# A reordered start, reordered steps, and a unit's scores and outputs placed on either side of one product

## The chip, the cores and the metric

The kernel runs on one core of a Trainium2 chip. The metric is the device time of one execution in microseconds. Three runs of the kernel before gave 498.42 (median), 497.5 and 498.45.

## The reference, cut to what matters

Two stages follow each other. The first is a linear attention with a decaying state, for 4 sequences of 768 tokens and 8 heads of 48 channels:

```python
for t in range(S):
    cur = einsum('bhd,bhe->bhde', u[None] * kt, vt)
    y[:, :, t] = einsum('bhd,bhde->bhe', rt, state + cur)
    state = w[None, :, :, None] * state + einsum('bhd,bhe->bhde', kt, vt)
```

The second takes its output as x (3072 tokens of 384 channels) and computes g = elu(x @ w_in) with 2048 hidden channels, and then g @ w_out. All is in float32.

## The kernel before, in words

**Units and layers.** The tokens are cut into chunks of 128. A *unit* (n, b) is chunk n (0 to 5) of sequence b (0 to 3). In a unit the recurrence is written as matrix products: scores (k by r, both scaled by powers of w, masked), the diagonal with u, outputs (scores by v, plus r by the state) and the state that is handed on. The four units of a chunk give the 512 columns of x for a *layer* n of the second stage. A layer has 16 steps f, one for each 128 hidden channels: `hidden` multiplies x by w_in (L1198), `negative` and `elu` apply the nonlinearity, `split_g` splits g, and `project` multiplies by w_out (L1254; L1241 in the last layer). Float32 accuracy is kept by splitting x, g and the weights into a high part in a fast format and the rest, so that each product is three matmuls for each of three chunks, nine of 512 columns.

**Ahead of the branch.** `prepare` loads w and u and the first r, k and v, runs some matmuls on ones (`warm`, L486), turns w into a column by small matmuls (`by_channels`, L490, copied at L495), finds its smallest and largest value (L109, L110), from which a flag says whether the fast path is allowed (L111, L113), and forms the powers of w (L132). These instructions are put in order by the framework's planner. All engines then read the flag and branch.

**START.** In the fast path the order is written out by hand: each engine executes its instructions in the order in which the program issues them, and `START` is the list of short names that `start` goes through, for layer 0's own units and the first weights. For instance `Lk:3` loads k of unit 3, `rud:1` forms r u k of unit 1 on VectorE (L730, L731; without the d on POOL), `sum` sums it (L742), `krd` or `kr` multiplies k by its decays (L749), `Tr` and `Tk` transpose on TensorE (L635), `dr`, `dra`, `dk`, `tka` take the transposes out of PSUM, `A` is the scores (L772), `m0` and `m1` their masking (L694), `tl`, `tla`, `tld` copy the tails of v (L840), `vd` and `vdd` form v times the diagonal (L852), `O` and `V` are outputs (L869, L879), `xh` and `xl` split them into x (L888, L890), `wm` is warming matmuls (L500), and `H:0`, `H:1` are the first half (256 columns) of the first two products by w_in. `Lw` loads a tile of weights.

**The weights** come as float32 and are rounded by integer steps: `wd` (L574) and `lb` (L580) on ScalarE, `ma` (L588) and `mb` (L596), called merges here, on VectorE, the cast `sp` (L616) on ScalarE, the rests `r3` and `r4` (L626) on POOL. In layer 0 every step does this for the tile of two steps later.

**The steps.** `step` goes through `FIRST` in layer 0 and `LATER` in all others. Names with a last hexadecimal digit belong to a unit's *stage*: a unit of the next layers starts every four steps, and the digit says in which step of its life (4 to 11 for units of chunk 1, 4 to 9 for the others) the operation is issued. `ru` and `kr` and `sum` are as above; `t` transposes blocks on VectorE (L647), `m` moves them through DRAM (L656, L661), `br` (POOL, L670) and `bk` (ScalarE, L679) take them; units of chunk 1 use TensorE (`T`, `dr`, `tka`) instead. `D` puts the diagonal into the scores' tile (POOL, L976), `A` is the scores and the states' products (L921, L935), `pa` and `pb` copy the two halves of the scores under the mask (VectorE, L983), `ss` forms the two state sums (L945, L948), `Y` is the outputs (L999, L1007), `xy` (ScalarE, L1018), `xa` (VectorE, L1027), `xh` (ScalarE, L1034) and `xl` (L1036) bring them into x, `sw` decays the state (POOL, L951), `G` fills x by DMAs (L1112), and `rk` and `v` ask for the inputs of the unit after next. `proj` is the product by w_out of g of two steps before (of one step before up to step (1,3), so that step (1,4) has none). Behind the last one of a layer VectorE transposes the banks with the results (L1262).

Scores and outputs of a unit use the same two PSUM banks in turn, so outputs wait until the masked scores and the state sums have been taken out. All loads and stores are issued by SP, in order.

Of the kernel before, what the change touches and what calls it, by code (L numbers as in the profile page):

```python
# [18 lines left out]
B, H, S, D = 4, 8, 768, 48  # L19
# [13 lines left out]
FILL = DP - D  # L33
FILLS = [slice(i * DP + D, (i + 1) * DP) for i in range(2)]
W_LOW, W_HIGH = 0.8, 1.2
WARM = 6
EARLY = (1, 4)

DEEP, WIDE = 3, 2

START = """
inv tb ub Lv:1 Lk:3 wm:4 kt Tr:0 rud:1 kr:1 Tr:1 Tk:0 tl:1 dra:1 Lr:3 rud:0 Lw:0 dr:0 sum:1 sum:0 Tk:1 tka:1
dk:0 S:1 wd:0 tla:0 A:1 A:0 Tr:3 rud:3 Lk:2 Lr:2 kr:3 m0:1 m1:1 Tr:2 Tk:3 Lw:2 m1:0 vdd:1 rud:2 O:1 Lw:1 kr:0
m0:0 tka:3 vd:0 O:0 V:0 kr:2 Tk:2 Lv:3 wd:1 dr:3 lb:0 dr:2 Lw:4 sum:2 lb:1 sum:3 ma:0 xh:0 V:1 Lw:5 mb:0 Lw:3
A:3 ma:1 xh:1 xl:1 Lv:2 xl:0 tka:2 mb:1 m1:3 S:3 tla:2 S:0 lb:2 m0:3 tld:3 vdd:2 A:2 Ln:1 m1:2 vd:3 O:3 sp:1
S:2 wd:2 sp:0 m0:2 O:2 V:3 xh:3 V:2 wm:1 Lw:6 Ln:0 rsd:1 xh:2 ht rsd:2 rsd:0 xl:3 H:0 Lw:7 xl:2 Lw:8 H:1 wm:2
"""

FIRST = """
D9 ma rud8 rka ru4 wd lb hid A9 bk7 kr8 mb T8 neg m6 sum6 Ya sum8 t5 xya sp pa9 xaa kr4 br6 xha elu va dr8 pb9 r3 gh tka8 ss9 xlda D7 Gb swb proj gl Lw r4  # L50
"""
LATER = """
hid t5 Y9 A8 br7 pa8 D6 proj rud4 xy9 neg xa9 elu pb8 xh9 gh bk7 kr4 m5 ss8 xl9 rk8 gl v9 G9 sum5 sw9
"""


class Kernel:
# [12 lines left out]
    def prepare(self, ctx):  # L70
        nc, tc = self.nc, self.tc
        cp = ctx.enter_context(tc.tile_pool(name="cp", bufs=1))

        self.rev = cp.tile([P, H, DP], F32, tag="rev", name="rev")
        self.state = [cp.tile([P, HP, DP], F32, tag=f"state{b}", name=f"state{b}") for b in range(B)]
        early = self.rev.rearrange("p h d -> p (h d)")
        w_row = early[0:1, 0:DM]
        nc.sync.dma_start(w_row, self.w.rearrange("(o h) d -> o (h d)", o=1))

        self.w_col = w_col = cp.tile([P, 8 * HP], F32, tag="w_col", name="w_col")[:, :HP]  # L80
        nc.vector.memset(w_col, 1.0)

        self.slots = [
            (
                cp.tile([P, H, DP], F32, tag=f"r_t{i}", name=f"r_t{i}"),
                cp.tile([P, H, DP], F32, tag=f"k_t{i}", name=f"k_t{i}"),
                cp.tile([P, H, DP], F32, tag=f"v_t{i}", name=f"v_t{i}"),
            )
            for i in range(2)
        ]  # L90
        self.ident = cp.tile([P, P], F32, tag="ident", name="ident")
        make_identity(nc, self.ident)
        ones = early[:, DM:]
        nc.vector.memset(ones, 1.0)
        self.raw = {}
        for b in range(2):
            self.raw[0, b] = self.slots[b]
            self.clear_pads(self.slots[b])
        self.load_rk(0, 0, (0,))
        self.u_b = cp.tile([P, H, D], F32, tag="u_b", name="u_b")  # L100
        self.u_row, self.one = early[DP : DP + 1, 0:DM], ones[DP : DP + 1, :]
        nc.sync.dma_start(self.u_row, self.u.rearrange("(o h) d -> o (h d)", o=1))
        self.load_rk(0, 0, (1,))
        self.load_rk(0, 1)
        self.load_v(0, 0)


        lim = self.lim = cp.tile([1, 48], F32, tag="lim", name="lim")[:, 0:4]
        nc.vector.tensor_reduce(lim[:, 0:1], w_row, axis=AX.X, op=ALU.min)  # L109
        nc.vector.tensor_reduce(lim[:, 1:2], w_row, axis=AX.X, op=ALU.max)  # L110
        nc.vector.tensor_single_scalar(out=lim[:, 2:3], in_=lim[:, 0:1], scalar=W_LOW, op=ALU.is_ge)  # L111
        self.flag = cp.tile([1, 1], I32, tag="flag", name="flag")
        nc.vector.scalar_tensor_tensor(  # L113
            self.flag, lim[:, 1:2], W_HIGH, lim[:, 2:3], op0=ALU.is_le, op1=ALU.mult
        )

        self.warm(WARM, w_row, ones)


        self.mask = cp.tile([P, P], F32, tag="mask", name="mask")  # L120
        nc.gpsimd.memset(self.mask, 1.0)
        nc.gpsimd.affine_select(
            out=self.mask, in_=self.mask, pattern=[[1, P]], compare_op=ALU.is_gt,
            fill=0.0, base=0, channel_multiplier=-1,
        )
        for t in self.state:
            nc.gpsimd.memset(t, 0.0)
        self.pw = cp.tile([P, HP, P + 1], F32, tag="pw", name="pw")
        nc.vector.memset(self.pw[:, :, 0:1], 1.0)

        for a in range(HP):
            nc.vector.tensor_tensor_scan(  # L132
                self.pw[:, a, 1 : P + 1], w_col[:, a : a + 1].to_broadcast([P, P]), ones,
                1.0, op0=ALU.mult, op1=ALU.mult,
            )

        self.pairs = []
        for k in range(NF + 1):
            self.pairs.append([
                cp.tile([P, self.count(k), DM], F32R, tag=f"{n}{k}", name=f"{n}{k}")  # L140
                for n in ("wh", "wl")
            ])
# [335 lines left out]
    def warm(self, times, w_row, ones):  # L478

        with self.tc.tile_pool(name="ps_w", bufs=1, space=PSUM) as ps:  # L480
            junk = ps.tile([P, P], F32, tag="junk", name="junk")
            col = ps.tile([P, HP], F32, tag="col", name="ps_col")
            for i in range(times):
                if i == 2:
                    self.by_channels(col, w_row, ones[0:1, 0:1], self.w_col)
                self.nc.tensor.matmul(junk, lhsT=ones, rhs=ones, start=True, stop=True)  # L486

# [804 lines left out]
@with_exitstack  # L1292
def rwkv_elu_ffn(ctx: ExitStack, tc: tile.TileContext, r, k, v, w, u, w_in, w_out, out):
    nc = tc.nc
    kn = Kernel(tc, r, k, v, w, u, w_in, w_out, out)
    kn.prepare(ctx)

    near_one = nc.values_load(kn.flag, min_val=0, max_val=1)
    with tc.If(near_one > 0) as cmp:
        kn.arm(general=False)  # L1300
    with cmp.Else():
        kn.arm(general=True)
# [30 lines left out]
```

## Time and profile before

| what | before |
| --- | --- |
| median of 3 runs | 498.42 us |
| profiled execution | 498.74 us |
| its span | 497.0 us |
| TensorE matmul busy | 482.9 us (97%) |
| VectorE busy | 288.7 us (58%) |
| ScalarE busy | 253.7 us (51%) |
| POOL busy | 152.7 us (31%) |
| all DMA queues, share of 16 engines | 40.3% and 0.7% |

The span runs from the first to the last instruction of the profiled execution; 1.74 us lie around it. Busy shares are means over stages with different limits: VectorE is busy for 9 tenths and more in some slices up to 110 us and for 4 to 6 tenths later. A busy TensorE includes the time in which a matmul passes through its pipeline, so the starts of the matmuls are read where times between them matter.

### The profile page before, as it was taken

The page shows a single profiled execution, that of the slowest core. Times are in us where ns is not written, and L with a number is a line of the kernel's source. Part 1 is how long each engine was busy: PE and PEld are TensorE (multiplying, and loading weights), DVE is VectorE, ACT ScalarE, POOL GpSimd, SP SyncE. Part 2 cuts the span into 40 slices and gives each one's busy share as a digit, 9 for nine tenths or more (in the row PEclk, how much of TensorE's full clock was granted, in tenths as well). Part 3 has the DMA queues.
Part 4 walks back from the last instruction along what each step waited for, and adds up shares of the span by engine and source line. Part 5 has one row for each costly group of instructions (what it writes and reads, how often), then busy time and mean ns, then how long its engine had stood idle before and what let it go on. Part 6 is the DMA issues. An engine that isn't in the chain of part 4 may idle for free.

```text
span 497.0 us, 11551 instructions
## 1 busy us (share of the span) xinstructions
PE 482.9 (97%) x4650; PEld 398.7 (80%) x4650; DVE 288.7 (58%) x506; ACT 253.7 (51%) x454; POOL 152.7 (31%) x169
## 2 busy tenths in 40 slices
PE   8899999999999999999999999999999999999995
PEld 7787877777878888788888788888788888899995
DVE  6988898995565455554454654554754633433332
ACT  2459988863543544444444444445435435444442
POOL 4457769573331322322313303313302201000000
PEclk9999999999999999999999999999999999999998
DMA  7977666733444533434434434534434300020002
GB/s 161 237 176 179 188 176 165 171 103 96 122 95 115 141 74 85 119 90 120 122 84 98 113 76 120 139 64 104 119 73 124 94 17 11 11 54 0 1 0 71
DMA packets 109955, 51.06 MB, mean 103 GB/s; under 512 B 89026, under 2 KB 105796, under 8 KB 109892
## 3 DMA queue, kind: packets, MB, share of 16 engines
q1 hardware_dynamic: 109892, 50.22, 40.3%
q8 instruction: 39, 0.64, 0.6%
q14 instruction: 24, 0.20, 0.1%
HBM read 35.13 MB, written 13.11 MB: 97 GB/s over the span
## 4 chain that ended last, share of the span: by engine, by line
PE 78%; DVE 11%; ACT 4%; issue 2%; POOL 2%; DMA 1%; SPq 0%; DVEq 0%; ACTq 0%
PE ps_h L1198 32%; PE ps_acc L1254 27%; PE ps_acc L1241 7%; DVE wide L596 3%; DVE wide L588 3%; PE ps_y L999 2%; PE ps_a L921 2%; PE ps_y L1007 2%; PE ps_a L935 1%; ACT wh L616 1%; DVE ps_h L1213 1%; PE ps_y L869 1%; DVE g L1221 1%; ACT g L1219 1%; DMA r_t<-in_r_dram 1%
## 5 line engine op out<-in xcount | busy, mean ns | idle before, releaser
L1198 PE MATMUL ps_h<-x,wh 128*128 128x512 f32 (+1 forms) x588 | 174.6, 386 | 0.4 <-DMA x<-x 0.4
L1254 PE MATMUL ps_acc<-g,wh 128*128 128x512 f32 x480 | 167.1, 401 | 1.4 <-DVE g L1221 0.8
L1198 PEld LDWEIGHTS ps_h<-x,wh 128*128 128x128 f32 x588 | 109.5, 188 | 22.2 <-issue 0.8
L1213 DVE SCALAR_TENSOR_TENSOR ps_h<-g,ps_h 128x512 f32<-128x512 f32 x96 | 66.5, 693 | 93.3 <-ACT g L1208 93.3
L1198 PE MATMUL ps_h<-x,wl 128*128 128x512 f32 (+1 forms) x294 | 108.8, 387 | 0.8 <-POOL wl L626 0.8
L1254 PEld LDWEIGHTS ps_acc<-g,wh 128*128 128x128 f32 x480 | 89.9, 188 | 23.6 <-DVE stage L1262 1.8
L1207 ACT ACTIVATE g<-ps_h 128x512 f32<-128x512 f32 x96 | 57.6, 600 | 82.6 <-PE ps_h L1198 82.5
L1219 ACT CAST g<-ps_h 128x512 fp32r<-128x512 f32 x96 | 56.3, 587 | 76.7 <-DVE ps_h L1213 76.7
L1254 PE MATMUL ps_acc<-g,wl 128*128 128x512 f32 x240 | 93.8, 391 | 0.0
L1221 DVE TENSOR_TENSOR g<-ps_h,g 128x512 fp32r<-128x512 f32 x96 | 66.2, 689 | 46.2 <-ACT g L1219 45.9
L1198 PEld LDWEIGHTS ps_h<-x,wl 128*128 128x128 f32 x294 | 55.0, 188 | 12.9 <-POOL wl L626 2.1
L1208 ACT ACTIVATE g<-g 128x512 f32<-128x512 f32 x96 | 60.7, 633 | 3.1
L749 POOL TENSOR_TENSOR k_t<-k_t,rev 128x384 f32<-128x384 f32 x22 | 24.5, 1117 | 99.2 <-DVE ru L731 92.6
L1254 PEld LDWEIGHTS ps_acc<-g,wl 128*128 128x128 f32 x240 | 45.1, 188 | 8.1
L1036 POOL TENSOR_TENSOR x<-x_f,x 128x512 fp32r<-128x512 f32 x16 | 20.7, 1295 | 91.2 <-ACT x L1034 91.2
L626 POOL TENSOR_TENSOR wl<-wide,wh 128x384 fp32r<-128x384 f32 x29 | 35.8, 1254 | 16.1 <-ACT wh L616 16.1
L983 DVE COPY_PREDICATED a<-mask,ps_a 128x256 f32<-128x256 int32 x40 | 17.8, 444 | 31.8 <-PE ps_a L935 30.8
L1018 ACT COPY x_f<-ps_y 128x256 f32<-128x256 f32 x40 | 12.9, 374 | 43.9 <-PE ps_y L1007 43.9
L1241 PE MATMUL ps_acc<-wh,g 128*128 128x384 f32 x128 | 35.0, 337 | 0.0
L670 POOL TENSOR_TENSOR rk<-rk,pw 128x512 f32<-128x512 f32 x16 | 19.0, 1189 | 35.3 <-DMA rk<-blocks 33.5
L1241 PEld LDWEIGHTS ps_acc<-wh,g 128*128 128x128 f32 x128 | 23.4, 188 | 0.6
L976 POOL TENSOR_TENSOR a<-ident_h,diag 128x512 f32<-128x512 f32 x20 | 21.6, 1080 | 6.7 <-DVE diag L742 6.3
(127 smaller groups left out, 478.7 us busy)
## 6 DMA issues: line engine op xcount, KB each, us to landing
blocks<-tb SPq DMA_DIRECT2D x64, 128.0 KB
rk<-blocks SPq DMA_DIRECT2D x16, 512.0 KB
stage<-in_moe_w_out_dram SPq DMA_DIRECT2D x16, 384.0 KB
stage<-in_moe_w_in_dram SPq DMA_DIRECT2D x32, 144.0 KB
r_t<-in_r_dram SPq DMA_DIRECT2D x22, 192.0 KB
k_t<-in_k_dram SPq DMA_DIRECT2D x22, 192.0 KB
v_t<-in_v_dram SPq DMA_DIRECT2D x22, 192.0 KB
out_dram<-stage SPq DMA_DIRECT2D x80, 48.0 KB
```

What stands on the lines that cost most here:

```text
L626: (eng or self.nc.gpsimd).tensor_sub(lo, a, hi.bitcast(F32))
L749: (eng or self.nc.gpsimd).tensor_mul(k, k, self.rev[:, :, 0:D])
L976: self.nc.gpsimd.tensor_mul(un["a"], self.ident_h.unsqueeze(1).to_broadcast([P, H, DP]), un["diag"].unsqueeze(2).to_broadcast([P, H, DP]),)
L1036: (eng or nc.gpsimd).tensor_sub(x[:, 1], xf, x[:, 0].bitcast(F32))
L1198: self.nc.tensor.matmul(ph[:, part], lhsT=a[:, c * P : (c + 1) * P], rhs=x[:, c, part], start=(i == 0), stop=(i + 1 == len(todo)),)
L1207: nc.scalar.activation(g, ph, AF.Relu, scale=-1.0)
L1208: nc.scalar.activation(g, g, AF.Exp, scale=-1.0)
L1213: self.nc.vector.scalar_tensor_tensor(ph, g, -1.0, ph, op0=ALU.add, op1=ALU.max)
L1219: nc.scalar.copy(part, g)
L1221: nc.vector.tensor_sub(part, g, self.g[n, f][2].bitcast(F32))
L1241: self.nc.tensor.matmul(self.acc[n][b][:, 0:DM], lhsT=a[:, at], rhs=w, start=(f == 0 and i == 0), stop=(f == NF - 1 and i == 2),)
L1254: self.nc.tensor.matmul(self.acc[n][c], lhsT=w[:, c * P : (c + 1) * P], rhs=g, start=(f == 0 and i == 0), stop=(f == NF - 1 and i == 2),)
```

## The change

In `prepare` the order is now the written one too, `warm` stands ahead of the compare and the flag, and has 4 matmuls on ones instead of 6, two of them ahead of the column of w. `START`, `FIRST` and `LATER` hold other orders. In `LATER` the scores `A8` stand ahead of the product by w_in (`hid`) and the outputs `Y8` behind it in the same step; before, scores stood behind the product, and outputs (`Y9`) behind the product of the next step. The block transposes and moves (`t`, `m`) and `bk` go one stage earlier, `rk` one stage later.

```diff
--- before.py
+++ after.py
@@ -33,24 +33,27 @@
 FILL = DP - D
 FILLS = [slice(i * DP + D, (i + 1) * DP) for i in range(2)]
 W_LOW, W_HIGH = 0.8, 1.2
-WARM = 6
+WARM = 4
+FIRST_WARM = 2
 EARLY = (1, 4)
 
 DEEP, WIDE = 3, 2
 
 START = """
-inv tb ub Lv:1 Lk:3 wm:4 kt Tr:0 rud:1 kr:1 Tr:1 Tk:0 tl:1 dra:1 Lr:3 rud:0 Lw:0 dr:0 sum:1 sum:0 Tk:1 tka:1
-dk:0 S:1 wd:0 tla:0 A:1 A:0 Tr:3 rud:3 Lk:2 Lr:2 kr:3 m0:1 m1:1 Tr:2 Tk:3 Lw:2 m1:0 vdd:1 rud:2 O:1 Lw:1 kr:0
-m0:0 tka:3 vd:0 O:0 V:0 kr:2 Tk:2 Lv:3 wd:1 dr:3 lb:0 dr:2 Lw:4 sum:2 lb:1 sum:3 ma:0 xh:0 V:1 Lw:5 mb:0 Lw:3
-A:3 ma:1 xh:1 xl:1 Lv:2 xl:0 tka:2 mb:1 m1:3 S:3 tla:2 S:0 lb:2 m0:3 tld:3 vdd:2 A:2 Ln:1 m1:2 vd:3 O:3 sp:1
-S:2 wd:2 sp:0 m0:2 O:2 V:3 xh:3 V:2 wm:1 Lw:6 Ln:0 rsd:1 xh:2 ht rsd:2 rsd:0 xl:3 H:0 Lw:7 xl:2 Lw:8 H:1 wm:2
+Lk:3 inv Lv:1 Lr:3 tb ub kt rud:1 Tr:0 sum:1 krd:1 Tr:1 tl:1 Tk:0 dra:1 rud:0 dr:0 vdd:1 Tk:1 tka:1 Lw:0 dk:0
+S:1 wd:0 lb:0 tld:0 A:1 Lr:2 A:0 wm:2 Lk:2 Tr:3 sum:0 rud:3 m0:1 m1:1 Tr:2 kr:3 Lw:1 Tk:3 m0:0 rud:2 m1:0 kr:0
+O:1 kr:2 O:0 vd:0 Lw:2 sum:2 V:0 Tk:2 dr:3 Lv:3 Lw:4 dr:2 tka:3 Lw:3 lb:1 V:1 ma:0 mb:0 wd:1 A:3 ma:1 tka:2
+xh:1 sum:3 xl:1 Lv:2 xh:0 Lw:6 mb:1 xl:0 lb:2 sp:1 m1:3 S:0 m0:3 tl:3 Lw:5 S:3 tla:2 A:2 vdd:2 m1:2 Ln:1 vd:3
+Ln:0 S:2 m0:2 O:3 O:2 V:3 wd:2 V:2 sp:0 ht xh:3 rsd:2 Lw:7 rsd:0 xh:2 rsd:1 wm:2 H:0 xl:3 H:1 Lw:8 xl:2
 """
 
 FIRST = """
-D9 ma rud8 rka ru4 wd lb hid A9 bk7 kr8 mb T8 neg m6 sum6 Ya sum8 t5 xya sp pa9 xaa kr4 br6 xha elu va dr8 pb9 r3 gh tka8 ss9 xlda D7 Gb swb proj gl Lw r4
+
+D9 lb ma ru4 hid wd Ya A9 neg rud8 t5 mb xya xaa sp elu ss9 kr8 kr4 pb9 bk7 rkb pa9 sum8 xha sum7 gh Lw xlda T8 dr8 gl br7 r3 r4 D7 m6 tka8 Gb swb vb proj
 """
 LATER = """
-hid t5 Y9 A8 br7 pa8 D6 proj rud4 xy9 neg xa9 elu pb8 xh9 gh bk7 kr4 m5 ss8 xl9 rk8 gl v9 G9 sum5 sw9
+
+A8 pb8 ss8 br7 rk9 hid pa8 neg rud4 kr4 xy9 Y8 elu t4 sw8 xa9 v9 bk6 gh gl xh9 xl9 G9 m4 proj D6 sum5
 """
 
 
@@ -108,13 +111,14 @@
         lim = self.lim = cp.tile([1, 48], F32, tag="lim", name="lim")[:, 0:4]
         nc.vector.tensor_reduce(lim[:, 0:1], w_row, axis=AX.X, op=ALU.min)
         nc.vector.tensor_reduce(lim[:, 1:2], w_row, axis=AX.X, op=ALU.max)
+
+        self.warm(WARM, w_row, ones)
+
         nc.vector.tensor_single_scalar(out=lim[:, 2:3], in_=lim[:, 0:1], scalar=W_LOW, op=ALU.is_ge)
         self.flag = cp.tile([1, 1], I32, tag="flag", name="flag")
         nc.vector.scalar_tensor_tensor(
             self.flag, lim[:, 1:2], W_HIGH, lim[:, 2:3], op0=ALU.is_le, op1=ALU.mult
         )
-
-        self.warm(WARM, w_row, ones)
 
 
         self.mask = cp.tile([P, P], F32, tag="mask", name="mask")
@@ -481,7 +485,7 @@
             junk = ps.tile([P, P], F32, tag="junk", name="junk")
             col = ps.tile([P, HP], F32, tag="col", name="ps_col")
             for i in range(times):
-                if i == 2:
+                if i == FIRST_WARM:
                     self.by_channels(col, w_row, ones[0:1, 0:1], self.w_col)
                 self.nc.tensor.matmul(junk, lhsT=ones, rhs=ones, start=True, stop=True)
 
@@ -1293,7 +1297,8 @@
 def rwkv_elu_ffn(ctx: ExitStack, tc: tile.TileContext, r, k, v, w, u, w_in, w_out, out):
     nc = tc.nc
     kn = Kernel(tc, r, k, v, w, u, w_in, w_out, out)
-    kn.prepare(ctx)
+    with tc.manual_schedule():
+        kn.prepare(ctx)
 
     near_one = nc.values_load(kn.flag, min_val=0, max_val=1)
     with tc.If(near_one > 0) as cmp:
```

## Rows read from the trace of the kernel before

**Rows 1.** The page's part 1: busy us (share of span) and instructions of each engine.
```profile
PE 482.9 (97%) x4650; PEld 398.7 (80%) x4650; DVE 288.7 (58%) x506; ACT 253.7 (51%) x454; POOL 152.7 (31%) x169
```

**Rows 2.** Chain that ended last, three stretches: start us, us, what.
```profile
59.73 1.70 DVE wide L588
...
68.48 0.87 ACT wh L616 x2
...
72.22 0.88 DVE wide L588
...
131.55 2.04 PE ps_h L1198 x9
...
141.54 0.14 issue
```

**Rows 3.** Timeline of TensorE: start us, us, engine, line, op, tiles, count [idle before].
```profile
35.09 0.36 PE L1198 MATMUL ps_h<-x,wh 128*128 128x256 f32 x1
...
57.78 1.52 PE L1198 MATMUL ps_h<-x,wh 128*128 128x512 f32 x6
...
78.97 1.30 PE L1198 MATMUL ps_h<-x,wh 128*128 128x512 f32 x5
```

**Rows 4.** Timeline of all engines, ahead of the branch.
```profile
1.15 2.50 PE L486 MATMUL junk<-rev 128*128 128x128 f32 x10 [1.15 <-DVE pw L129]
...
4.44 0.15 DVE L495 COPY w_col<-ps_col 48x4 f32<-48x4 f32 x1 [1.09 <-PE ps_col L490]
```

**Rows 5.** Timeline of VectorE in the start.
```profile
9.62 0.56 DVE L731 TENSOR_TENSOR ru<-ru,k_t 128x384 f32<-128x384 f32 x1
11.01 0.69 DVE L694 TENSOR_TENSOR rk<-ps_rT,pw 128x512 f32<-128x512 f32 x1 [0.83 <-PE ps_rT L635]
```

**Rows 6.** Timeline of TensorE, transposes of r in the start.
```profile
9.91 1.91 PE L635 MATMUL ps_rT<-ident,r_t 128*128 128x128 f32 x8
...
15.75 1.09 PE L635 MATMUL ps_rT<-ident,raw 128*128 128x128 f32 x8
```

**Rows 7.** Windows: us, busy (instructions) by engine, PEclk, DMA share, GB/s.
```profile
0.00:10.00 10.00, 8.31 (x43) 6.73 (x44) 6.58 (x23) 1.95 (x3) 4.47 (x26) 1.00 0.74 146
10.00:20.00 10.00, 8.56 (x103) 7.76 (x103) 8.98 (x16) 4.53 (x10) 6.86 (x9) 1.00 0.87 220
```

**Rows 8.** Timeline of VectorE, step (0,1).
```profile
43.27 0.45 DVE L983 COPY_PREDICATED a<-mask,ps_a 128x256 f32<-128x256 int32 x1 [0.94 <-POOL a L976]
```

**Rows 9.** Timelines around two units' scores: TensorE and VectorE.
```profile
193.51 0.69 PE L921 MATMUL ps_a<-rk,tb 48*64 48x64 f32 x32
...
194.59 0.50 PE L1254 MATMUL ps_acc<-g,wh 128*128 128x512 f32 x1
...
194.78 0.45 DVE L983 COPY_PREDICATED a<-mask,ps_a 128x256 f32<-128x256 int32 x1 [1.91 <-PE ps_a L935]
...
210.85 0.61 PE L1198 MATMUL ps_h<-x,wh 128*128 128x512 f32 x2
...
211.65 0.69 DVE L1221 TENSOR_TENSOR g<-ps_h,g 128x512 fp32r<-128x512 f32 x1 [0.65 <-ACT g L1219]
...
216.96 0.35 DVE L948 TENSOR_TENSOR sw<-mid,ps_a 128x192 f32<-128x192 f32 x1
```

**Rows 10.** Timeline of VectorE, a unit's fourth step in the first layer.
```profile
75.56 0.69 DVE L1221 TENSOR_TENSOR g<-ps_h,g 128x512 fp32r<-128x512 f32 x1 [0.87 <-ACT g L1219]
```

**Rows 11.** Timeline of TensorE, start of the second layer.
```profile
116.41 0.70 PE L1198 MATMUL ps_h<-x,wh 128*128 128x512 f32 x2 [0.37 <-DMA x<-x]
```

**Rows 12.** Waits: engine line waited for: us in total, times, longest us.
```profile
ACT x_f L1018 <- PE ps_y L1007: 43.9, 17, 3.8
...
POOL rk L670 <- DMA rk<-blocks: 33.5, 15, 4.8
...
PE ps_y L999 <- DVE mid L945: 0.7, 1, 0.7
...
PE ps_acc L1254 <- DVE stage L1262: 0.6, 3, 0.2
```

## The prediction

> **What bounds the kernel now.** I read the busy shares first, then the chain of work that ended last, then the waits, and last the timelines where the chain leaves TensorE. The reader is to see that TensorE is busy for 97% of the span [rows 1], but that the span has three parts with different limits. From about 120 us on, the products by w_in and by w_out follow each other in the chain, nine matmuls in 2.04 us each time [rows 2]: no other engine can shorten this part, except where TensorE waits. Between 45 and 113 us the chain runs through VectorE and ScalarE: in each step the word merge (L588, L596) releases the cast of the weights (L616) [rows 2], that the split of g or x, and that the next merge. Four steps, in which one unit of attention passes, take 78.97 - 57.78 = 21.19 us there [rows 3]; eight products are 16.3 of it, the rest is attention and waits. Before 35 us the chain changes between VectorE and TensorE, and VectorE's queue is the longer one.
>
> The profiled execution took 498.74 us: the span of 497.0 and 1.74 around it. The median of the runs is 0.32 lower. I sum against 498.74 and take 0.3 off at the end.
>
> **The change part by part.**
>
> *Ahead of the branch.* Ten junk records of 0.25 us stand ahead of the column products of w, and VectorE's copies of the column idle 1.09 us for them [rows 4]; without that they could start at 3.35. Two junk matmuls instead of five are four records, so the column products can start 1.5 us sooner, at about 2.2, when w is just in (the reductions that read it end at 3.35, and take no part in the copies' data). So the 1.09 us go. Behind the copies come now the compare, the flag and a small memset, which stood elsewhere: at most 0.15 each by the copy's own row, 0.3 together as the sum takes it. Gain for the powers of w and the branch: 0.8 us. The junk matmuls left out give nothing themselves, since TensorE waits for the branch.
>
> *START.* I count VectorE's queue up to the last masked scores, on which the last outputs wait. The list is the same but for three entries. Unit 1's k times its decays comes from POOL: 0.56 us, as the product of the same size [rows 5]. Unit 0's tails come from ScalarE and unit 3's go to POOL, which cancels. Added: 0.56, and up to 1.0 if POOL works beside it as it does beside other products of the start. Taken away: 0.83 of idle before the first product of r [rows 5], where VectorE waits for the transposes; sum and decays of unit 1 stand there now. So the last masked scores end 0.8 + 0.83 - 0.56 = 1.1 us sooner. Behind them stand the same outputs, and 4 warming records instead of 2 and 4: 0.2 us less by the spacing of [rows 6]. Together 1.3 us sooner at the rest of the first product by w_in.
> What could eat this are the transfers. 1.46 MB move in the first 10 us [rows 7] (146 GB/s), seven blocks of 0.197 MB and a little; v of unit 1 is now the seventh instead of the sixth, an estimate of 9.5 us, and its first reader on VectorE comes at about 11. The k and r of unit 3 follow as before, those of unit 2 change places, a tile of w_out comes ahead of one of w_in that is used no sooner. Price of the order of loads: nothing; if it is wrong, up to the 1.1 us.
> The four warming matmuls ahead of the inverse tables go. They stand in a wait for VectorE, so their time gives nothing; what their absence may do is the second rival.
>
> *First layer's steps (FIRST).* In step 1 VectorE stands 0.94 us before the masked scores, for the diagonal from POOL [rows 8], with elu queued behind. After, elu (0.6) and the two sums of states (0.35 each [rows 9]) stand ahead: 1.3 us of work in a wait of 0.94. Gain 0.9.
> For the later steps I compare VectorE's order entry by entry. The loop merge, cast, split, merge stays. Masked scores behind elu and sums take the same time in all. The sum of r u k goes from a unit's third step, where it lay beside the cast, to the fourth, where VectorE idles 0.87 us for the cast of g [rows 10]. Nothing either way. POOL's second low part r4 goes ahead of the diagonal and the decay of the state. That changes what lies beside two merges of a unit, and merges take from 0.88 to 1.70 us in this layer [rows 2]. The two are now near the middle; I take 0, with bounds of 0.4 either way for each: 2 x 0.4 x 3.5 units = -2.8 to +2.8.
> The r, k and v of the unit after next are asked for a step later, past fills and blocks on SP. No step of before waits for such a load by the view of the waits, and each still has at least two steps, over 8 us, until its first reader. Nothing.
>
> *Turn to the second layer.* Its first product waits 0.37 us for the fill of x [rows 11]. A unit's scores now stand ahead of it, 1.08 us (193.51 to 194.59 [rows 9]), and cover that. Gain 0.4.
>
> *Later steps (LATER).* Scores before and outputs behind the product by w_in are as many small matmuls as before, with again four changes to and from the large ones: no time on TensorE by itself. One stall goes: in step (1,5), where no product by w_out lies between, the outputs waited 0.7 us for VectorE's state sum [rows 12], with products of the next unit and an elu between the halves of the masked scores. Those stand behind now. Gain 0.7. At three turns of a layer TensorE waits for the transposed banks, 0.6 in all [rows 12]. There ScalarE had waited for the outputs (2.6 us in the mean of 17, same rows) with the negative part of h queued behind, so VectorE came late to the transposes. The outputs come a step earlier now. Gain 0.6, between 0 and 0.6.
> The new wait is that of the outputs on the masked scores of the same step; the product by w_out queues behind it. I place it in the step whose product starts at 210.85 [rows 9]. The scores start there: 210.94 with the gap of such a change. VectorE could begin 1.27 later (193.51 to 194.78), at 212.21, and its split of g from 211.65 frees it at 212.25 to 212.34. Two halves of 0.45 and two sums of 0.35 end at 213.9, and TensorE starts 0.14 later [rows 2], 214.04. The product by w_in lies at 212.02 to 214.06 or 214.17. So the outputs are just in time: cost 0, with nothing to spare.
> The blocks of the next unit go out a step sooner in the order, but behind elu, and ScalarE's copy of them stands a step sooner, ahead of the cast of g. POOL waited for this data 2.2 us in the mean and at most 4.8 [rows 12]; if ScalarE waits as long, g is that late, and is used two steps later, over 8 us. Nothing.
>
> **Sum.** 1.3 + 0.9 + 0.4 + 0.7 + 0.6 = 3.9 us. 498.74 - 3.9 = 494.8 for such an execution, 494.5 for the median.
>
> **Rivals.**
> *1. The outputs wait for VectorE in every unit.* For it: the 0.7 us of (1,5), the one place of before with this order, and a slack of nothing. Against it: two products and an elu stood between there, 1.75 us, and are gone. If each of 16 units waits 0.7, the time is 494.5 + 0.7 + 11.2 = 506.4; at 0.3 per unit it is slower than before, that is once the masked scores end 0.4 us behind my place for them.
> *2. The start isn't shortened.* With data that come no sooner, 494.5 + 1.1 = 495.6. Or with a slow TensorE: the eight transposes from 9.91 start 0.21 us apart, those from 15.75 0.12 apart [rows 6], while the granted clock reads 1.00 all along [rows 7], so only the spacing tells; TensorE had been busy nearly throughout from 1.15 on. With less work ahead the slow spacing may last longer; 5 us more of it cost 5 x (1 - 0.12/0.21) = 2.1 us where nothing covers: 496.6, and 497.7 with both.
> The Trainium skill ("TensorE: Matmul & The Clock Gate", Part 1) has the array start at half clock and rise only with sustained activity, and so speaks against fewer warming matmuls; the spacing in rows 6 agrees.
> *3. The merges meet POOL otherwise.* At the bounds above: 491.7 or 497.3, and another 1.5 if more merges than two change. For it: one instruction takes 0.88 or 1.70. Against it: POOL's block of work stays whole, only its inside changes.
>
> **How the numbers follow.** The forecast, 494.5 and itself between 493 and 496: 0.49. Rival 1: 0.11. Rival 2, 495.6 to 498: 0.18. Rival 3 fast, 490.5 to 493: 0.11; slow, 496.5 to 499.5: 0.11. The range 491.2 to 498.8 leaves out rival 1 and the ends of rival 3. A measurement here tells 0.2%, 1 us, from no change; faster is below 497.4. That holds for the forecast, the fast rival and nearly all of rival 2, 0.76; of the others 0.11 lies within and 0.13 above.
>
> **What would show it.** Right: the copies of the column at 3.4 and the powers of w near 4.1; the rest of the first product by w_in near 33.8; step (1,0) without a wait for x, L999 without one for L945; four steps of the first layer still near 21 us. Wrong: L999 behind L983 in many units; transposes 0.21 us apart after 13 us; merges slower in the mean; VectorE waiting for v in the start.

## The result, and the profile after

The kernel after took 492.16 us (median of 4 runs, 491.91 to 492.53), the one before 498.44 beside it: ratio 0.9881, 95% interval 0.9865 to 0.9897. Forecast were 494.5 and a range of 491.2 to 498.8. The profiled execution took 492.12 with a span of 490.3; 498.74 and 497.0 before.

Line numbers of the kernel after are those of before plus 4 (plus 3 up to L110). Part 1 of its page, against [rows 1], then TensorE's waits (us in total, times, longest): only such of the start are left. Those for the fill of x, the state sum and the transposed banks [rows 11, 12] are gone, and so are two waits for g and three for POOL's low part of the weights in the first layer, 0.8 us in all each.

```profile
PE 479.5 (98%) x4640; PEld 396.6 (81%) x4640; DVE 286.2 (58%) x507; ACT 253.4 (52%) x453; POOL 151.6 (31%) x169
```
```profile
PE junk L490 <- DVE rev L97: 1.2, 1, 1.2
PE ps_kT L639 <- POOL k_t L753: 1.0, 1, 1.0
PE ps_a L776 <- POOL rk L696: 0.7, 1, 0.7
PE ps_u L509 <- DVE pw L136: 0.6, 1, 0.6
PE ps_a L776 <- DVE x L894: 0.4, 1, 0.4
PE ps_y L873 <- DVE a L698: 0.3, 1, 0.3
PE ps_a L776 <- DVE rk L698: 0.2, 1, 0.2
```

Where the time went is read from the starts of the products by w_in on TensorE. The table gives how much sooner a product starts in the profile after; the last column is against a second profile of the unchanged kernel before (run e8 below, 497.31 us).

| product of step | before | after | lead | lead against e8 |
| --- | --- | --- | --- | --- |
| (0,2) | 42.85 | 41.10 | 1.75 | 1.76 |
| (0,5) | 57.78 | 55.84 | 1.94 | 1.82 |
| (0,9) | 78.97 | 76.25 | 2.72 | 1.90 |
| (0,13) | 100.07 | 96.63 | 3.44 | 1.98 |
| (0,15) | 111.80 | 108.12 | 3.68 | 2.29 |
| (1,2) | 127.30 | 122.99 | 4.31 | 2.93 |
| (1,6) | 145.32 | 139.90 | 5.42 | 4.04 |
| (2,6) | 221.64 | 215.74 | 5.90 | 4.48 |
| (3,6) | 297.91 | 291.58 | 6.33 | 4.93 |
| (4,6) | 374.16 | 367.39 | 6.77 | 5.33 |
| (5,15) | 482.73 | 475.97 | 6.76 | 5.32 |

From step (1,6) on the lead grows at the turns of the layers alone. Two things were not in the sum: 0.7 us in each of two units of the first layer, and more at every wait of the later layers than the view of the waits had listed.

The first layer's four steps took 20.41 and 20.38 us where [rows 3] had 21.19. In the windows of these two stretches (us; busy and count of PE, PEld, DVE, ACT, POOL; PEclk, DMA share, GB/s) TensorE is busy for all but 0.2 us. In e8, the second profile of the kernel before, the same stretches take 20.49 and 20.46, so there too TensorE, and not VectorE's loop, was nearly the bound.

```profile
55.84:76.25 20.41, 20.22 (x210) 16.16 (x208) 18.93 (x26) 18.18 (x32) 16.38 (x14) 1.00 0.69 186
76.25:96.63 20.38, 20.23 (x210) 16.16 (x208) 18.90 (x26) 18.20 (x32) 16.34 (x14) 1.00 0.62 171
```

What held TensorE up was the split of x on VectorE (L1036). The timelines of VectorE and POOL before show it at 1.57, and behind it stands the split of g (L1221), for which a product by w_out waits 0.43; the rows are one from each engine's timeline, and the wait:

```profile
70.05 1.57 DVE L1036 TENSOR_TENSOR x<-x_f,x 128x512 fp32r<-128x512 f32 x1
...
69.08 2.00 POOL L626 TENSOR_TENSOR wl<-wide,wh 128x384 fp32r<-128x384 f32 x2 [1.44 <-ACT wh L616]
...
72.28 0.73 PE L1254 MATMUL ps_acc<-g,wh 128*128 128x512 f32 x2 [0.43 <-DVE g L1221]
```

After, the same split takes 0.69, and it is POOL's pair of low parts that is longer:

```profile
67.95 0.69 DVE L1040 TENSOR_TENSOR x<-x_f,x 128x512 fp32r<-128x512 f32 x1 [0.52 <-ACT x L1038]
...
67.06 2.46 POOL L630 TENSOR_TENSOR wl<-wide,wh 128x384 fp32r<-128x384 f32 x2 [1.44 <-ACT wh L620]
```

The first low part of a pair takes 1.02. Before, the split starts 0.97 behind the pair, about when POOL begins the second low part, and it ends 0.54 after that one: it has waited for it. After, it starts 0.89 behind the pair, ahead of the second low part, and that one waits. My theory from here on (P): of two such instructions the one that gets in first goes through and the other stands still, and the change moved the split to the right side of a near tie. The recorded starts don't tell who won a tie: before, the split's lies 1 to 9 ns ahead of that of the second low part both times that it lost.

The Trainium skill ("SBUF — State Buffer", section "SBUF: two separate sides") states just this: VectorE with two inputs in SBUF and a GpSimd operation that reads SBUF share a pair of ports, and whichever starts first has it for the whole instruction. The rows agree as far as they resolve it: 0.69 where the split starts 0.08 ahead, 1.57 in the tie.

### The profile page after: what moved, and what is told of

It reads as the page before. It is cut to its first block, busy times and chain, and to the rows that moved or that the text cites. A ratio compares the mean times of both kernels' runs of the same rounds, so it can differ in the third digit from the quotient of the medians.

```text
span 490.3 us, 11493 instructions
## 1 busy us (share of the span) xinstructions
PE 479.5 (98%) x4640; PEld 396.6 (81%) x4640; DVE 286.2 (58%) x507; ACT 253.4 (52%) x453; POOL 151.6 (31%) x169
## 4 chain that ended last, share of the span: by engine, by line
PE 81%; DVE 6%; POOL 3%; DMA 3%; SPq 2%; ACT 2%; issue 1%; DVEq 0%; ACTq 0%; POOLq 0%
PE ps_h L1202 36%; PE ps_acc L1258 29%; PE ps_acc L1245 7%; PE ps_y L1003 2%; DMA k_t<-in_k_dram 2%; PE ps_a L925 2%; POOL wl L630 2%; DVE wide L600 2%; DVE wide L592 2%; PE ps_y L1011 2%; PE ps_a L939 2%; DMA stage<-in_moe_w_out_dram 1%; SPq L205 1%; PE ps_y L873 1%; ACT wh L620 1%
## 5 line engine op out<-in xcount | busy, mean ns | idle before, releaser
L1258 PE MATMUL ps_acc<-g,wh 128*128 128x512 f32 x480 | 164.0, 396 | 0.0
L1202 PEld LDWEIGHTS ps_h<-x,wh 128*128 128x128 f32 x588 | 108.2, 188 | 21.4
L630 POOL TENSOR_TENSOR wl<-wide,wh 128x384 fp32r<-128x384 f32 x29 | 33.8, 1190 | 15.9 <-ACT wh L620 15.9
L980 POOL TENSOR_TENSOR a<-ident_h,diag 128x512 f32<-128x512 f32 x20 | 23.7, 1185 | 2.5 <-PE ps_a L925 2.5
L600 DVE SCALAR_TENSOR_TENSOR wide<-stage,wide 128x768 int32<-128x768 int32 (+1 forms) x17 | 21.3, 1256 | 0.5
L1245 PE MATMUL ps_acc<-wl,g 128*128 128x384 f32 x64 | 21.5, 336 | 0.0
```

What stands on the lines that cost most here:

```text
L600: self.nc.vector.scalar_tensor_tensor(a, high, -(2**31), a, op0=ALU.bitwise_and, op1=ALU.bitwise_or)
L630: (eng or self.nc.gpsimd).tensor_sub(lo, a, hi.bitcast(F32))
L980: self.nc.gpsimd.tensor_mul(un["a"], self.ident_h.unsqueeze(1).to_broadcast([P, H, DP]), un["diag"].unsqueeze(2).to_broadcast([P, H, DP]),)
L1202: self.nc.tensor.matmul(ph[:, part], lhsT=a[:, c * P : (c + 1) * P], rhs=x[:, c, part], start=(i == 0), stop=(i + 1 == len(todo)),)
L1245: self.nc.tensor.matmul(self.acc[n][b][:, 0:DM], lhsT=a[:, at], rhs=w, start=(f == 0 and i == 0), stop=(f == NF - 1 and i == 2),)
L1258: self.nc.tensor.matmul(self.acc[n][c], lhsT=w[:, c * P : (c + 1) * P], rhs=g, start=(f == 0 and i == 0), stop=(f == NF - 1 and i == 2),)
```

## Experiments

**e1: the sum back in its step.** The sum of r u k had gone from a unit's third step, where it delayed the addition to x, to the fourth. Here it stands in the third again.

```diff
-D9 lb ma ru4 hid wd Ya ... sum8 xha sum7 gh
+D9 lb ma ru4 hid wd sum6 Ya ... sum8 xha gh
```


> The kernel after, with the sum of r u k back in a unit's third step, ahead of the addition of the outputs to x. Theory P: the unpredicted 0.75 us per unit of the first layer came from the split of x on VectorE, which now starts just ahead of POOL's second low part (0.69 us) instead of just behind it (1.57). Put back, the sum makes the split late again: L1040 with x in the first layer back to 1.1 to 1.57, four steps 21.0 to 21.2 us instead of 20.4, total 493.7 to 494.7. Rival M: the order of the merges and of POOL's low parts made it; then four steps stay near 20.4 and the total near 492.2.

Measured: 491.85, ratio 0.9888 (0.9872 to 0.9903); four steps took 20.52 and 20.38, and the split 0.69. So the sum's step alone is not the cause. But the theory's condition was not met: the sum stands between the two merges there, the second merge took 1.30 instead of 1.65, and the split started at 68.09, still first. The last unit shows a split that is clearly second: it starts 0.51 behind a low part of POOL and ends 0.55 behind that one's end, as the split of 1.57 did.

```profile
108.24 1.05 DVE L1040 TENSOR_TENSOR x<-x_f,x 128x512 fp32r<-128x512 f32 x1
107.73 1.01 POOL L630 TENSOR_TENSOR wl<-wide,wh 128x384 fp32r<-128x384 f32 x1 [1.97 <-ACT wh L620]
```

**e2: the sum alone, in the kernel before.**

```diff
-... T8 neg m6 sum6 Ya sum8 ... xha elu va
+... T8 neg m6 Ya sum8 ... xha elu sum7 va
```


> The kernel before, with the sum of r u k one step later (behind elu) and nothing else changed. Theory P: the split of x (L1036) falls to 0.69 in the first layer, four steps take 20.4 to 20.6 us instead of 21.2, the total is 496.3 to 497.0. Rival M: no change, 498.4 and 21.1 to 21.2.

Measured: 497.44, ratio 0.9995 (0.9986 to 1.0004). The timeline agrees with P: the split is at 0.69 in all units, and starts 0.88 behind POOL's pair.

```profile
69.99 0.69 DVE L1036 TENSOR_TENSOR x<-x_f,x 128x512 fp32r<-128x512 f32 x1 [0.52 <-ACT x L1034]
...
69.11 2.46 POOL L626 TENSOR_TENSOR wl<-wide,wh 128x384 fp32r<-128x384 f32 x2 [1.44 <-ACT wh L616]
```

The product of (0,15) starts 1.43 sooner than in the profile before; 0.32 of it is lost at the turn, where the wait for the fill of x is 0.7 instead of 0.37, and the execution took 497.14. The median did not move, against what I expected. Either other things had become slower, or the median of before holds executions in which the split is fast anyway. Its 23 runs beside e1 to e4 lie between 496.4 and 498.8, the 12 of e2 between 496.8 and 497.7, the 4 of the kernel after within 0.6. Hence e8.

**e3: POOL's second low part behind the diagonal, as before.**

```diff
-... gl br7 r3 r4 D7 m6 tka8 Gb swb vb proj
+... gl br7 r3 D7 m6 tka8 Gb swb vb r4 proj
```


> The kernel after, with POOL's second low part r4 behind the diagonal and the decay of the state again, as before. Theory P: the split of x meets the low parts in another step, so nothing changes there: total 492.2 within 0.5, four steps 20.4. Rival M (POOL's place beside two merges of a unit gave the gain): back to 21.1 per four steps, total near 494.

Measured: 491.44, ratio 0.9872 (0.9857 to 0.9887), four steps 20.4. Merges changed places with each other beside POOL (the one at 54.5 took 1.16 instead of 1.68, the next 1.67 instead of 1.17) and nothing came of it: my third rival, in which merges that meet POOL otherwise decide, falls.

**e4: the outputs made late.** The first rival with its condition made true.

```diff
-A8 pb8 ss8 br7 rk9 hid pa8 neg rud4 kr4 ...
+A8 rud4 pb8 ss8 br7 rk9 hid pa8 neg kr4 ...
```


> The kernel after, with the two products of r, u and k for the next unit (two of about 0.57 us on VectorE) ahead of the masked scores of the later layers instead of behind them. The masked scores end near 207.8 for outputs that start at 208.39, a slack of about 0.45 with 0.14 from end to start. Theory S (my first rival, with its condition made true): the outputs come 0.6 to 0.7 late in each of 15 units, total 492.2 + 9 to 10.5 = 501 to 503, slower than before. Rival: the outputs don't hang on VectorE's place there, or the wait is won back by the next products: under 494.

Measured: 498.58, ratio 1.0018 (1.0009 to 1.0027). The rival's mechanism is real: the two products (0.55 and 0.56) put the masked scores and state sums 1.07 later and cost 0.48 in most units, 7.2 in all by the starts of the products, and all of the change's gain is gone. It is less than the 9 to 10.5 that I expected. Its timelines of VectorE and TensorE, and a row of its waits:

```profile
210.59 0.35 DVE L952 TENSOR_TENSOR sw<-mid,ps_a 128x192 f32<-128x192 f32 x1
...
211.09 0.65 PE L1003 MATMUL ps_y<-rk,state 48*64 48x64 f32 x14 [0.17 <-DVE sw L952]
```
```profile
PE ps_y L1003 <- DVE sw L952: 2.6, 12, 0.7
```

In the kernel after the second state sum, which the outputs wait for in e4, ends at 207.42, and the outputs start at 208.39, behind the last matmul of the product and without a wait: 0.97 behind the sum. In e4 they start 0.15 behind it, so the slack is 0.82. Of the 0.48 half, 0.24, is the later start of the outputs; the rest is that they take 1.34 instead of 1.10 to the next product.

```profile
207.07 0.35 DVE L952 TENSOR_TENSOR sw<-mid,ps_a 128x192 f32<-128x192 f32 x1
...
208.08 0.39 PE L1202 MATMUL ps_h<-x,wl 128*128 128x512 f32 x1
208.39 0.46 PE L1003 MATMUL ps_y<-rk,state 48*64 48x64 f32 x16
```

**e5: the sum where it delays the split.** As e1, but behind the second merge.

```diff
-D9 lb ma ru4 hid wd Ya A9 neg rud8 t5 mb xya xaa ... xha sum7 gh
+D9 lb ma ru4 hid wd Ya A9 neg rud8 t5 mb sum6 xya xaa ... xha gh
```


> The kernel after, with the sum of r u k in a unit's third step as in the run before, but this time right behind the second merge, so that the addition to x, the cast of x and the split of x on VectorE all come 0.55 us later (the first run had it between the merges, where the second merge gave 0.35 of it back and the split still started first). Theory P, mended: what counts is only who starts first, the split of x (67.95 in the kernel after) or POOL's second low part (68.04). Now the split starts at 68.4 to 68.6, behind: it takes 1.3 to 1.6 us, four steps of the first layer 20.9 to 21.2, total 493.3 to 494.3. Rival N: the split is late, but VectorE has slack enough (it idles 0.3 to 0.5 us three times per unit), four steps stay at 20.4 and the total below 492.4.

Measured: 493.48 (492.21 to 494.59), ratio 0.9912 (0.9897 to 0.9927). The profiled execution (492.21) holds both outcomes, a unit apart, with the split 0.97 behind POOL's pair each time:

```profile
67.81 0.69 DVE L1040 TENSOR_TENSOR x<-x_f,x 128x512 fp32r<-128x512 f32 x1
...
66.84 2.55 POOL L630 TENSOR_TENSOR wl<-wide,wh 128x384 fp32r<-128x384 f32 x2 [1.45 <-ACT wh L620]
...
88.23 1.57 DVE L1040 TENSOR_TENSOR x<-x_f,x 128x512 fp32r<-128x512 f32 x1
...
87.26 2.00 POOL L630 TENSOR_TENSOR wl<-wide,wh 128x384 fp32r<-128x384 f32 x2 [1.44 <-ACT wh L620]
```

Around the second unit the product of (0,11) starts 0.18 sooner than in the kernel after, that of (0,12) 0.52 later. The median is as P expected; the split was not behind in every unit, as I had thought, but in a tie. By these starts an execution that loses both ties would take near 492.9, so the runs at 493.5 to 494.6 hold something more, which no profile here shows.

**e6: START as before, all else after.**

> The kernel after with START as before; prepare and both lists of steps stay. The rest of the first product came 1.75 us sooner, of which about 1.0 stood already at the first current of unit 1. Theory A: START gave the other 0.75, and nothing wins it back later: total 492.9. Rival: prepare's lead is lost in the old START, which waits for loads, so that it gave all: 493.9. Second rival: the steps of the first layer take a later start up in VectorE's idle time: 492.2.

Measured: 493.08, ratio 0.9905 (0.9889 to 0.9920). The product of (0,1) starts 0.56 later than after, that of (0,13) 0.59, that of (5,15) 0.65: nothing wins a late start back. The median is nearest to theory A. The trace doesn't show START's part: eight profiles with the new start begin the first product between 30.57 and 31.59, and here it is 31.39.

**e7: LATER as before, all else after.**

> The kernel after with LATER as before. By the anchors of the two traces the later steps gave 0.8 (turn to the second layer) + 1.1 (step (1,5)) + 1.2 (turns of the layers) = 3.1 us. Theory A: all of it is LATER's: total 495.2 (494.8 to 495.5). Rival: 0.8 and part of 1.2 come from the first layer's order or from a better place of the transfers, then 493.3 to 494.5.

Measured: 495.24, ratio 0.9947 (0.9934 to 0.9961). In the profile the product of (0,15) starts 0.22 sooner than after and that of (5,15) 3.41 later. Theory A: the gain of the later layers is LATER's, some 3.1 to 3.6 us.

**e8: the kernel before, unchanged.**

> The kernel before, unchanged. 23 executions of it lie between 496.4 and 498.8, those of the kernel after within 0.6. Theory P: before, the split of x and POOL's second low part start within 0.01 us of each other (70.05 and 70.06), so each execution decides anew which goes first, in three units, 0.7 us each: a profile of an execution near 497 shows the split at 0.69 in one or two of three units and four steps of 20.5 there, one near 498.7 none. Rival: the spread comes from elsewhere (start, transfers), and the split takes 1.57 in every execution.

Measured: 498.02, ratio 1.001 (0.9997 to 1.0023). The profiled execution took 497.31, and here the split is fast in all units, at the same 0.97 behind the pair:

```profile
69.95 0.69 DVE L1036 TENSOR_TENSOR x<-x_f,x 128x512 fp32r<-128x512 f32 x1
...
68.98 2.55 POOL L626 TENSOR_TENSOR wl<-wide,wh 128x384 fp32r<-128x384 f32 x2 [1.44 <-ACT wh L616]
```

The wait for g at 72.28 isn't there, and the product of (0,13) starts at 98.61 instead of 100.07. 498.74 - 497.31 = 1.43, the two units. So P holds: the same kernel wins both ties in one execution and loses both in another. It would also explain e2, if a good part of the runs of before have the fast split already. The two units make 1.43 us of the spread of 2.4; the rest stays open.

**e9: the kernel after, unchanged.**

> The kernel after, unchanged. Theory P: its split of x starts 0.09 us ahead of POOL's second low part, and that seldom turns: 491.8 to 492.5 in all executions, the split at 0.69 to 0.8 in every unit. Rival: the race turns here as well in some executions, then single ones at 492.9 and 493.6.

Measured: 491.64 (491.23 to 491.98), ratio 0.9869 (0.9853 to 0.9884); the split at 0.69 in all four units but the last (0.79). P. It is as fast as e3 within what these runs tell, so e3 is no better version.

**e10: FIRST as before, all else after.**

> The kernel after with FIRST as before. Theory P: the lead of the start (1.75) and of the later steps (3.1) stays; of FIRST's part there are 0.3 to 0.5 us that don't hang on the race (0.1 at the product at 57.8, the rest in the last steps of the layer), and 0, 0.72 or 1.45 us by one, two or three units in which the race is won or lost: 492.5 to 494.1, spread over more than 1 us. Rival: FIRST gave 1.9 us whatever the race: 494.0 with a spread under 0.7.

Measured: 492.89 (492.61 to 493.66), ratio 0.9899 (0.9883 to 0.9915). The time fits P, but not for its reason: in the profile the split is fast in all units. What is lost is a new wait of 1.45 us, scores of the unit at step (0,5) waiting for ScalarE; the product of (0,6) is 1.25 late by it against the kernel after, that of (0,13) 0.42, the last 0.74. With this START the old FIRST meets something else, so this run doesn't price FIRST. (Line numbers here are those of before plus 3, in e11 plus 2.)

```profile
59.37 0.69 PE L924 MATMUL ps_a<-rk 48*64 48x64 f32 x32 [1.45 <-ACT rk L726]
```

**e11: `prepare` as before, all else after.**

> The kernel after with prepare as before (planner's order, six matmuls on ones, the column behind the second pair of them). Old START cost 0.64 by the anchors of its trace, of 1.75 in all. Theory A: prepare gave the other 1.1: total 493.0 to 493.4. Rival: loads set the start, so that prepare's lead is lost in START: under 492.5.

Measured: 492.03, 0.39 above e9 beside it; ratio 0.9880 (0.9865 to 0.9896). Theory A fell, and the time is the rival's. `prepare` brings the powers of w and the first transposes 1.1 us sooner (7.35 instead of 8.48), and START loses nearly all of it in these two profiles: the timelines of VectorE and POOL, first after, then e11:

```profile
10.91 1.29 DVE L856 TENSOR_TENSOR vd<-v_t,diag 128x288 f32<-128x288 f32 x1
12.12 0.56 DVE L860 TENSOR_TENSOR vd<-v_t,diag 128x96 f32<-128x96 f32 x1
...
10.40 0.26 POOL L844 COPY raw<-v_t 128x96 f32<-128x96 f32 x1 [4.36 <-DMA v_t<-in_v_dram]
10.71 1.18 POOL L696 TENSOR_TENSOR rk<-rk,pw 128x512 f32<-128x512 f32 x1
```
```profile
11.94 0.71 DVE L854 TENSOR_TENSOR vd<-v_t,diag 128x288 f32<-128x288 f32 x1
12.58 0.25 DVE L858 TENSOR_TENSOR vd<-v_t,diag 128x96 f32<-128x96 f32 x1
...
11.10 1.24 POOL L694 TENSOR_TENSOR rk<-rk,pw 128x512 f32<-128x512 f32 x1 [0.80 <-ACT rk L693]
```

After, v of unit 1 lands at 10.4, POOL's product queues behind its copy, and VectorE's starts 0.20 behind that product: it stands for the rest of it. In e11 VectorE comes 0.84 behind it and stands only for the end. The product of the second half (k's decays) follows at 12.61 and at 12.75: of 1.03 us 0.14 are left. That hangs on when v lands. In e11 POOL's copy of v starts at 9.65; in e4, with the new `prepare` and the same START, it starts at 9.76, and there the product of the second half stands at 12.03, so 0.72 are left.

**e12: the four warming matmuls back.**

```diff
-Lk:3 inv Lv:1 Lr:3 tb ub kt rud:1 ...
+Lk:3 inv Lv:1 Lr:3 tb ub wm:4 kt rud:1 ...
```


> The kernel after with the four warming matmuls (eight records, 2.07 us before) back ahead of the inverse tables. In the kernel after TensorE works without a gap from 4.84 to 11.2, so they stand in no wait any more. Theory A: the eight transposes after them come 1.0 to 2.0 later, and the fast spacing begins at the same time or a little sooner, so that the rest of the first product comes 0.3 to 1.2 later: 492.4 to 493.4. Rival (my second one, the clock): the fast spacing begins much sooner with them, which wins back more than they take: at or below 491.8.

Measured: 492.98, 1.34 above e9; ratio 0.9900 (0.9882 to 0.9918). The transposes come 1.8 later than after (7.35, eight in 1.92), the first product by w_in 0.88 (32.02 instead of 31.14), and 0.43 later than in e9, the latest of the kernels with the new start. Theory A; the clock as a rival falls: TensorE's clock didn't rise sooner for the eight records more (10.42 here, 10.20 and 9.34 in the two profiles of the kernel after). TensorE's timeline:

```profile
6.42 2.08 PE L504 MATMUL ps_junk<-ident 128*128 128x128 f32 x8
...
9.14 1.67 PE L639 MATMUL ps_rT<-ident,r_t 128*128 128x128 f32 x8
```

## Why the prediction was right, and where its sum was not

The direction and the range held, and the time came out 2.3 us below the forecast. Against the profile on which I summed, 6.6 us went, and 3.9 were forecast.

- **Start: 1.3 forecast, 1.75 by the table.** The copies start at 3.15 (forecast 3.4), the scans at 3.78 (4.1), the rest of the first product near 33.3 (33.8). How it adds up was wrong. By the medians old START costs 0.9 to 1.4 (e6 against the two of the kernel after), old `prepare` at most 0.4 (e11); the sum had 0.8 for `prepare`. The price of the order of loads, set at nothing with v of unit 1 at 9.5, is the term that was wrong: POOL's copy of v starts at 9.76 in e4, 9.97 in e5, 10.14 in e7, 10.25 in e10, 10.40 in the kernel after and 10.42 in e3, all with the same start, and the first product follows in the same order at 30.57, 30.87, 30.91, 31.01, 31.14 and 31.16. (In e9, 10.33 and 31.59, 0.5 is lost later, at a wait for the split of x.) So 0.4 either way between two executions is no finding. The warming matmuls, which I gave nothing, stood in no wait any more (e12). Even before they stood in one for a part only: VectorE's work for the inverse tables ended at 8.06, and the matmul behind the warming started at 9.06.
- **Step (0,1): 0.9 forecast, 0.1 to 0.2 measured** (lead 1.75 to 1.94, or 1.82). VectorE's wait for the diagonal [rows 8] went, as I said, but no matmul waited for it: TensorE's timeline before has no wait between these two, so idle time of an engine that TensorE did not wait for was priced as a gain.

```profile
37.90 0.66 PE L635 MATMUL ps_kT<-ident,k_t 128*128 128x128 f32 x4 [1.06 <-POOL k_t L749]
...
65.03 0.97 PE L1198 MATMUL ps_h<-x,wl 128*128 128x512 f32 x3 [0.34 <-POOL wl L626]
```

- **First layer's loop: 0 forecast, 1.5 against the profile before, 0.2 against e8.** This is the step that failed: "nothing either way" for the sum of r u k. I looked for what it lay beside, not for what stood behind it: the addition, the cast and the split of x, and the split is what met POOL. The row of 1.57 for it was in the trace, beside rows of 0.69 of the same form, and I did not ask why. I did weigh merges against POOL, as rival 3, within its bounds, and those gave nothing (e3). Another 0.24 (0.31 against e8) comes between (0,13) and (0,15), where before the last low part of POOL is waited for and the outputs take 1.47 to the next product, 1.31 after; no run tests it.
- **Later layers: 1.7 forecast, 3.1 measured** (turn 0.63, step (1,5) 1.11, three turns 0.47, 0.44 and 0.43; e7 confirms the sum). All three mechanisms were right, and all three sizes too small in the same manner: I took the waits as the view lists them, 0.37, 0.7 and 0.2 each. What a wait costs is read from start to start. TensorE before, at a turn:

```profile
204.66 0.39 PE L1254 MATMUL ps_acc<-g,wh 128*128 128x512 f32 x1
205.24 0.50 PE L1254 MATMUL ps_acc<-g,wh 128*128 128x512 f32 x1 [0.20 <-DVE stage L1262]
205.58 0.39 PE L1254 MATMUL ps_acc<-g,wl 128*128 128x512 f32 x1
```

Matmuls start 0.23 apart there; these are 0.58 and 0.34 apart, so 0.35 + 0.11 = 0.46 is lost where the list has 0.20: the list counts from the end of a matmul, 0.39 behind its start, while one that needn't wait starts 0.23 behind the start of the one before, and the next matmul comes late too. At (1,5) the outputs themselves are also longer, 1.47 from their start to the next product instead of 1.09.

- **The new wait: nothing forecast, nothing found.** The outputs of all units start on time, with a slack of 0.82 by e4 where I had seen none. The masked scores start as placed, 1.32 behind the scores; but the outputs wait for the state sums, not for the second half that I let them wait for (in e4 they start 0.21 ahead of its end). At 0.3 per unit my rival was to be slower than before; e4 with 0.48 takes 1.05 us more than the runs of before beside it.
- **The slow TensorE (rival 2).** I read the granted clock as 1.00 throughout the start [rows 7]. But the trace's record of the clock begins at 12.01 us before, and the 1.00 of the window ahead of that is the lack of a record; at that moment the spacing falls from 0.21 to 0.11, as from the lower of the two levels, 1.2 GHz, to the upper. In the eight profiles with the new start it begins between 9.34 (e9) and 12.15 (e7), in seven of them ahead of 12.01 and in no order with the first product (31.59 and 30.91). So fewer warming matmuls didn't keep the clock low for longer, and the moment of its rise didn't set the start.
- **The baseline.** 1.43 us of the profile before were two lost ties. Its median holds some of them too (498.4, 497.5, 497.9 and 497.9 in four sets of runs), so of the ratio an unknown part, at most 1.4 us by this, is that the tie is gone; the rest, 5.2 us against e8, is `prepare`, START, FIRST and LATER. How often before loses the tie was not counted. That the time fell within the range is in part luck: a 0.9 that never came stands against 1.5 and 1.4 that were not in the sum.

## What to carry to other kernels

Where one instruction has two durations of the same form in a trace, look at what POOL and VectorE start within 0.1 us of it before pricing a move at nothing, and ask what is queued behind a moved instruction, not only what lies beside it. A spread of runs can be a sign of such a tie: 2.4 us before, 0.9 in e2, where the sum alone was moved. Ask of every wait that a change takes away whether the engine that bounds the stage waits for it. Price a wait of TensorE from start to start of its matmuls, not from the list of waits.

## What the runs showed of the hardware that was not expected

- A start 0.97 us behind POOL's pair went either way (0.69 or 1.57 for the same instruction, e5 and two profiles of before), 0.88 to 0.90 always first: under 0.1 us decided over 0.7 us of TensorE's time per unit. Within 9 ns the order of the recorded starts doesn't tell the winner: 9 ns ahead lost before, 2 ns behind won in e10.
- The instruction that gets in second pays: POOL's pair took 2.00 when it went first and 2.46 to 2.55 when VectorE did. A split that came second ended 0.55 behind the end of POOL's low part, whether it had started with that one (before) or 0.51 behind its start (e1).
- The record of TensorE's full clock begins at moments from 9.34 to 12.15 us in eight profiles with the same start, with TensorE busy nearly throughout from 1.15 on: eight transposes of k from 9.06 took 1.60 in one profile of the kernel after (10.20) and 1.18 in the other (9.34). Ahead of the first record of the clock a window reads 1.00 while the matmuls start 0.21 us apart, 0.11 later.
